# One fetch of v in place of three in the attention of a 12-chunk recurrent kernel, the other two layouts made by TensorE transposes and ScalarE copies

## The chip, the cores and the metric

The kernel runs on one core of a Trainium2 chip. The metric is the time of one execution in microseconds (us); the profile's span leaves out a little at both ends. Engines are named as in the profile: PE (TensorE products; PEld is its weight load), DVE (VectorE), ACT (ScalarE), POOL (GpSimd), SP (SyncE, which here only issues DMAs). Each works through its own list of instructions in a fixed order.

## What is computed

An attention with a recurrent state, over 4 x 8 = 32 heads, 768 time steps and head width 40, and behind it two dense blocks on the 4 x 768 x 320 result:

```python
for t in range(S):                                   # attention; S = 768, state is 40 x 40 per head
    y[:, :, t] = einsum('bhd,bhde->bhe', r_t, state)
    Sa = einsum('bhde,bhe->bhd', state, a_t)
    state = state*w_t - outer(Sa, b_t) + outer(v_t, k_t)
...
mixed = real(fft(fft(x, axis=1), axis=2)); u = x + mixed           # block 1
un = normalise(u); x = u + relu(un @ w_ch1) @ w_ch2                # 320 -> 1280 -> 320
...
u = x + (relu(x^T @ w_tok1) @ w_tok2)^T                            # block 2, over the 768 tokens
out = u + relu(u @ w_ch1) @ w_ch2                                  # 320 -> 1536 -> 320
```

## The kernel before

Attention is cut in 12 chunks (`NSC`) of 64 time steps. The 32 heads and one empty one stand in 11 groups (`NG`) of three, 3 x 40 = 120 partitions. Within a chunk the recurrence becomes products between matrices of 64 steps, and only the 40 x 40 state goes from chunk to chunk. The stages of a chunk, in the order in which `plan` lists them:

- `load`, `decay`, `kg`, `loada`, and `inv` for two chunks at a time: inputs, running products of w (DVE), the products of `am` (a under a head mask) with `bt`, and a triangular inverse of 47 DVE instructions. These run several chunks ahead. The inverse leaves through DRAM (`Ad`, `Md`) and comes back as `AT` and `Mst`.
- `merge`, `kbts`, `pts`: products and transposes that finish the inverse (tiles `mg`, `mc`) and lay out `kbt` and `PT`.
- `load2` (L336): fetches v with time on the partitions, into `LT[64:128]` and once more into `VZt[64:128]`. `load3` (L378): fetches r and v with the head's width on the partitions, into `VZd[:,:,1]`, and makes `rm`, r under three head masks (3 ACT instructions).
- `chain` (L342): the path from chunk to chunk. PE product x (from `RT` and `LT`) to `bdX`, product z, its copies by ACT into `VZt[0:64]`, product s (from `kbt` and `VZt`), and from it the state rows `LT[0:40]` of the next chunk.
- `outp` (L386): transposes st of the state, transposes zt of `VZt[0:64]` into `VZd[:,:,0]`, six products sc of `VZd` with `rm`, their masking, six products y with `kbt`, and `ys`.

`LT`, `r` and `kbt` have two buffers, `VZt`, `VZd` and `rm` one. PSUM has eight banks: 3 for chain and merge ('c'), 2 for kg and sc ('m'), 2 for transposes ('t'), 1 for y.

Among these run jobs for later blocks: the float64 weights are read as integers and turned into pairs of floats (`wdec`, `dec2`; tiles `da`, `mda`, `mdraw`, `mdt`), and behind the attention `fft`, `fft2` (tiles `Xh`, `Xl`, `psA`), the two MLP products (L1050, L1040), the token mixing and the last MLP (L1076).

What sets the order is a written list: `Plan.op` records every operation with an engine, what it reads and what it writes, and `Plan.emit` issues them in the sequence of `ORDER`, a string of base-36 numbers of operations. a suffix `:j` picks a PSUM bank, and an item `+m,bank,j` puts m fill-ins there: products of the identity with itself, whose result nothing reads (`warm`, L52). Every engine keeps to that order, so an instruction that waits holds up all that stands behind it on its engine. The semaphore waits themselves are put in by the framework from the tiles read and written.

Of the kernel before, what the change touches and what calls it, by code (L numbers as in the profile page):

```python
# [29 lines left out]
def layouts(r,k,v,w,a,b):  # L30
    def heads(x,fill=0.0):
        o=np.full((NH,768,D),fill,x.dtype); o[:32]=x.reshape(32,768,D); return o
    def rows(x,fill=0.0):
        h=heads(x,fill).reshape(NG,3,NSC,L,D)
        return np.ascontiguousarray(h.transpose(2,1,4,0,3)).reshape(NSC,120,NG,L)
    out={'rR':rows(r),'vR':rows(v)}
# [10 lines left out]
ATTN=['rR','vR','wR','aR','vT','bkR','hm']  # L47
# [49 lines left out]
class Attn:  # L97
# [232 lines left out]
    def load2(s,i):  # L330
        A=s.A
        s.dma(s.LT[i%2][64:128],A['vT'][i],[],[('LTv',i%2)],1.46,cost=.56,nd=4,bulk=1)
        if i+1<NSC: s.dma(s.VZt[64:128],A['vT'][i],[],['VZv'],1.46,cost=.56,nd=4,bulk=1)

    def chain(s,i):
# [25 lines left out]
        if i+1<NSC:  # L361
            nLT=s.LT[(i+1)%2]; PL=s.RT[(i+1)%NRT]
            for w in range(2):
# [5 lines left out]
                P.op('PE',.638,f,[('kbt',i%2),('VZ',2*w),('VZ',2*w+1),'VZv'],[kp,('LT',(i+1)%2,2*w),('LT',(i+1)%2,2*w+1)],alloc=h[0],cols=1651,cls=1)  # L369
# [8 lines left out]
    def load3(s,i):  # L378
# [3 lines left out]
        s.dma(s.VZd[:,:,1],A['vR'][i],[],['VZdv'],1.92,cost=.95,nd=88,bulk=1)  # L382
        for h in range(3): s.act(.77,s.rm[:,h],r,[('r',i%2),'hm'],[('rm',h)],scale=s.hm[:,h:h+1])

    def outp(s,i):
# [17 lines left out]
        for k in range(6):  # L403
# [4 lines left out]
            P.op('PE',.05+.305*m,f,[('VZd',x) for x in range(2)]+['VZdv']+[('rm',x) for x in range(3)],[ks,('sc',j,0),('sc',j,1)],alloc=hs[0],cols=720*m)  # L408
# [95 lines left out]
    def plan(s):  # L504
# [13 lines left out]
        for w in range(NSC):  # L518
            go(w,'merge','kbts','load2','load3','pts','chain','outp')
# [21 lines left out]
34 85:1 32 35 36 86 37 83 88:1 38 3a 8b:0 89 8y 8e:1 8c 39 3b 8f 3c 94 8k 3d 8l 93 3e 3g 92 3f 8m +7,y,0 95:0 3h 9h:1 96 3i 3j 9e:0 9i 8o 3m 9b:1 3n
9f 8q 3k 98:0 9c 3q 8p ce:1 e6 99 e4 8n 9k:1 3l 8j cg kt 87 cf 84 c1 8a 3o 9l 9p 9o 3p 3s c0 8d e0 dx c2 e1 9n 3t 8g e2 mv 97 3r 9g 3u 3x e5 hr 3v hx
3w 9t e3 hs 9q hw e7 ba ht e8 f3 e9 f2 hy hu b9 +12,y,0 ea:0 my bb 9r eb 9u bd 9v 9w +2,y,0 ej:1 9x ez 9y 9z 9s a0 a1 a2 bc a3 +2,y,0 ed:0 a4 fo a5
be:2 qp ee a6 bf a7 bg 48 ek bh aa bi a8 +2,y,0 ep:0 em:1 a9 eq bj ab ca +3,y,0 bk:0 ae hp ac +1,y,0 bl bm af eg:0 ad bn eh ag f4:1 f5 ah en f6 aj bo
# [763 lines left out]
```

## Time and profile before

| | |
|---|---|
| runs | 968.05, 970.48, 971.21 us; median 970.48 |
| the profiled execution | 967.6 us, its span 965.9 us |
| busy: PE, PEld, DVE, ACT, POOL | 910.0, 842.3, 712.1, 492.1, 374.8 us |
| instructions | 24197, of them 9641 PE products |
| moved by DMA | 146.15 MB, mean 151 GB/s |

The span falls into a start-up (0 to 90 us), the attention (90 to about 380 us), a passage through the FFTs (to 417 us) and the dense blocks (to the end). A busy share over the whole span mixes these; the rows further down are by stretch.

### The profile page before, as it was taken

How to read it: one execution, taken by the hardware profiler on the slowest of the kernel's cores; microseconds unless marked ns; L12 is line 12 of the kernel's file. 1: busy time of each engine (PE TensorE's matmuls, PEld its weight loads, DVE VectorE, ACT ScalarE, POOL GpSimd, SP SyncE). 2: the span in 40 equal slices, each digit the busy share in tenths (PEclk: the TensorE clock that was granted, in tenths of full speed). 3: DMA queues.
4: the chain of work that ended last, by engine and by line, in shares of the span. 5: the costliest groups of instructions: out<-in, count | busy, mean ns of one | idle time of the engine just before them, and what ended most of it. 6: DMA issues, size and time to landing. Idle time of an engine off the chain costs nothing. (4 is left out here: it accounts for less than half of the span.)

```text
span 965.9 us, 24197 instructions
## 1 busy us (share of the span) xinstructions
PE 910.0 (94%) x9641; PEld 842.3 (87%) x9641; DVE 712.1 (74%) x1543; ACT 492.1 (51%) x1068; POOL 374.8 (39%) x504
## 2 busy tenths in 40 slices
PE   7577899999999998799999999999999999999998
PEld 5467788888888887789898988999999999999998
DVE  7699679897968757998979656643786876766554
ACT  5265878888887765443434543323234343433422
POOL 6111614536354445444456553363233313132110
PEclk9688999999999999999999999999999999999999
DMA  9877778899867898755344524459452212303000
GB/s 214 168 150 175 173 160 191 195 220 206 190 168 173 203 268 264 269 177 173 119 163 127 171 75 127 130 154 390 137 182 74 79 52 75 101 1 99 1 29 29
DMA packets 153840, 146.15 MB, mean 151 GB/s; under 512 B 101695, under 2 KB 127359, under 8 KB 152959
## 3 DMA queue, kind: packets, MB, share of 16 engines
q1 hardware_dynamic: 143743, 117.64, 47.1%
q0 software_dynamic: 9984, 26.96, 9.1%
q8 instruction: 76, 1.25, 0.6%
q14 instruction: 37, 0.30, 0.1%
HBM read 96.22 MB, written 43.58 MB: 145 GB/s over the span
## 5 line engine op out<-in xcount | busy, mean ns | idle before, releaser
L1050 PE MATMUL hps<-cc,W1t 128*128 128x512 f32 x480 | 121.0, 396 | 0.9 <-DVE cc L1053 0.8
L1040 PE MATMUL acc<-W,cc 128*128 128x320 f32 x720 | 116.0, 310 | 0.0
L1040 PEld LDWEIGHTS acc<-W,cc 128*128 128x128 f32 x720 | 109.2, 188 | 4.7 <-ACT mdh L839 0.3
L1050 PEld LDWEIGHTS hps<-cc,W1t 128*128 128x128 f32 x480 | 87.8, 188 | 17.8 <-DVE cc L1053 1.1
L1100 POOL TENSOR_TENSOR C<-C,C 128x256 f32<-128x256 f32 x36 | 27.4, 760 | 173.2 <-DVE W1t L1093 115.5
L1052 ACT ACTIVATE cc<-hps 128x512 fp32r<-128x512 f32 x60 | 35.8, 596 | 106.5 <-PE hps L1050 106.5
L1053 DVE SCALAR_TENSOR_TENSOR cc<-hps,cc 128x512 fp32r<-128x512 f32 x60 | 41.3, 689 | 56.3 <-ACT cc L1052 56.1
L54 PE MATMUL warm<-ident 128*128 128x128 f32 x470 | 75.1, 298 | 4.1 <-ACT Xh L886 2.1
L226 POOL TENSOR_SCALAR_AFFINE_SELECT RT<-RT 64x384 f32<-64x384 f32 (+1 forms) x72 | 45.5, 651 | 78.1 <-ACT RT L136 73.6
L216 PE MATMUL kg<-am,bt 120*128 120x192 f32 x242 | 55.2, 363 | 19.3 <-ACT am L136 14.7
L54 PEld LDWEIGHTS warm<-ident 128*128 128x128 f32 x470 | 65.6, 206 | 6.6 <-ACT Xh L886 2.3
L417 POOL TENSOR_SCALAR_AFFINE_SELECT sc<-sc 64x384 f32<-64x384 f32 (+1 forms) x72 | 42.0, 583 | 73.4 <-ACT sc L136 67.2
L1094 DVE TENSOR_TENSOR C<-sb,C 128x256 f32<-128x256 f32 x108 | 44.2, 420 | 33.4 <-PE sb L1087 27.0
L1076 PE MATMUL acc<-v,W1t 128*128 128x320 f32 x432 | 67.4, 309 | 0.0
L1076 PE MATMUL acc<-vb,W1t 128*128 128x320 f32 x432 | 66.9, 309 | 0.0
L1092 ACT ACTIVATE W1t<-C 128x256 fp32r<-128x256 f32 x108 | 42.0, 413 | 45.5 <-DVE C L1094 36.6
L1076 PEld LDWEIGHTS acc<-v,W1t 128*128 128x128 f32 x432 | 63.7, 188 | 0.3 <-DVE W1t L1093 0.3
L1076 PEld LDWEIGHTS acc<-vb,W1t 128*128 128x128 f32 x432 | 63.7, 188 | 0.0
L216 PEld LDWEIGHTS kg<-am,bt 120*128 120x128 f32 x242 | 42.0, 206 | 24.5 <-ACT am L136 15.6
L1093 DVE SCALAR_TENSOR_TENSOR W1t<-C,W1t 128x256 fp32r<-128x256 f32 x108 | 46.6, 449 | 19.5 <-ACT W1t L1092 19.1
L407 PE MATMUL sc<-rm,VZd 120*128 120x192 f32 x264 | 56.7, 344 | 1.4 <-ACT sc L136 0.7
L860 POOL TENSOR_TENSOR mda<-mda,mdh 128x320 f32<-128x320 f32 (+2 forms) x32 | 31.4, 985 | 62.1 <-ACT mdh L857 47.0
(224 smaller groups left out, 2253.5 us busy)
## 6 DMA issues: line engine op xcount, KB each, us to landing
bt<-in_bkR_dram SPq DMA_DIRECT2D x12, 660.0 KB
mdraw<-in_moe_w_ch_dram SPq DMA_DIRECT2D x22, 320.0 KB
mdraw<-in_moe_w_ch_dram SPq DMA_DIRECT2D x16, 384.0 KB
dr_T<-Y SPq DMA_DIRECT2D x24, 256.0 KB
Z<-dr_T SPq DMA_DIRECT2D x6, 1024.0 KB
wS<-in_wR_dram SPq DMA_DIRECT2D x12, 335.2 KB
a<-in_aR_dram SPq DMA_DIRECT2D x12, 335.2 KB
RT<-a SPq DMA_DIRECT2D x36, 111.7 KB
```

What stands on the lines that cost most here:

```text
L54: for x in range(m): nc.tensor.matmul(t[:,128*(x%4):128*(x%4)+128],lhsT=ident,rhs=ident,start=True,stop=True)
L216: nc.tensor.matmul(ps[:,192*x:192*x+192],lhsT=bt[:,g+x].rearrange("p v t -> p (v t)"),rhs=am[:,:,g+x],start=True,stop=True)
L226: nc.gpsimd.affine_select(out=kv,in_=kv,pattern=[[0,3*m],[1,L]],compare_op=ALU.is_gt,fill=0.0,base=0,channel_multiplier=-1)
L407: for x,g in enumerate(gs): nc.tensor.matmul(ps[:,192*x:192*x+192],lhsT=VZd[:,g].rearrange("p v t -> p (v t)"),rhs=s.rm[:,:,g],start=True, ...
L417: nc.gpsimd.affine_select(out=o,in_=o,pattern=[[0,3*m],[-1 if rv else 1,L]],compare_op=ALU.is_gt,fill=0.0,base=L-1 if rv else 0,channel_mu ...
L1040: nc.tensor.matmul(s.pst(acc[x]),lhsT=a[:,sl],rhs=w2(w,m),start=(m==0 and n==0),stop=(m==MT-1 and n==2))
L1050: for n,(l,r) in enumerate(ops): nc.tensor.matmul(ps,lhsT=l,rhs=r,start=n==0,stop=n==7)
L1053: s.dve(.61,lambda: nc.vector.scalar_tensor_tensor(out=t["hl"][z],in0=s.pst(h),scalar=0.0,in1=t["hh"][z].bitcast(F32),op0=ALU.max,op1=ALU. ...
L1076: nc.tensor.matmul(s.pst(acc[x]),lhsT=a[:,sl],rhs=wv(w),start=(u==0 and y==0 and k==0),stop=(u==5 and y==1 and k==2))
L1092: s.act(256,lambda: nc.scalar.activation(out=Hh(y,c),in_=src(),func=AF.Relu),rd,[('Hh',z,y,c)],free=free)
L1093: s.dve(.33,lambda: V.scalar_tensor_tensor(out=Hl(y,c),in0=src(),scalar=0.0,in1=Hh(y,c).bitcast(F32),op0=ALU.max,op1=ALU.subtract),rd+[('H ...
L1094: def add(n,r,m,free): s.dve(.33,lambda: V.tensor_tensor(out=C(n),in0=R[r](),in1=C(m),op=ALU.add),[K[r],('C',m)],[('C',n)],free=free)
```

## The change

The input `vR` (v with the head's width on partitions) is no longer passed to the core, and `VZd[:,:,1]` is made on chip by a new stage `vts`: eleven TensorE transposes of `LT[64:128]` per chunk into a bank 't' (8 and 3 at a time), and two ACT copies from there. The second fetch of v into `VZt[64:128]` becomes two ACT copies from `LT[64:128]`, for every chunk but the last. `warm` issues up to four fill-ins as one product whose right side is the identity repeated along the columns, in the place of one product each. `ORDER` is another list: 4701 operations in place of 4654, with 213 fill-ins in 78 places in place of 235 in 84.

```diff
 def warm(nc,pool,ident,m):
     t=pool.tile([128,512],F32,tag="ps",name="warm")
-    for x in range(m): nc.tensor.matmul(t[:,128*(x%4):128*(x%4)+128],lhsT=ident,rhs=ident,start=True,stop=True)
+    for x in range(0,m,4):
+        k=min(4,m-x); nc.tensor.matmul(t[:,:128*k],lhsT=ident,rhs=ident.unsqueeze(1).to_broadcast([128,k,128]),start=True,stop=True)
...
     def load2(s,i):
         A=s.A
         s.dma(s.LT[i%2][64:128],A['vT'][i],[],[('LTv',i%2)],1.46,cost=.56,nd=4,bulk=1)
-        if i+1<NSC: s.dma(s.VZt[64:128],A['vT'][i],[],['VZv'],1.46,cost=.56,nd=4,bulk=1)
+        for h in range(2 if i+1<NSC else 0):
+            n=slice(17*h,17*h+17-h); s.act(.75,s.VZt[64:128,n],s.LT[i%2][64:128,n],[('LTv',i%2)],[('VZv',h)])
+
+    def vts(s,i):
+        nc=s.nc; P=s.P; LT=s.LT[i%2]; VZd=s.VZd
+        for g in range(0,NG,8):
+            m=min(8,NG-g); h=s.psum('t',[128,512],"vt"); kp=('ps',h[0])
+            def f(g=g,m=m,h=h):
+                ps=s.pst(h)
+                for x in range(m): nc.tensor.transpose(ps[:120,64*x:64*x+64],LT[64:128,3*(g+x):3*(g+x)+3].rearrange("p n d -> p (n d)"),s.ident[64:128,64:128])
+            P.op('PE',.065*m,f,[('LTv',i%2)],[kp,('VZdv',g//8)],alloc=h[0],cols=60*m,cls=3)
+            s.act(.05+.054*m,VZd[:,g:g+m,1],lambda h=h,m=m: s.pst(h)[:120,:64*m].rearrange("p (g t) -> p g t",t=L),[kp],[('VZdv',g//8)],free=[h[0]])
...
     def load3(s,i):
...
         s.dma(r,A['rR'][i],[],[('r',i%2)],1.3,bulk=1)
-        s.dma(s.VZd[:,:,1],A['vR'][i],[],['VZdv'],1.92,cost=.95,nd=88,bulk=1)
...
-            go(w,'merge','kbts','load2','load3','pts','chain','outp')
+            go(w,'merge','kbts','load2','vts','load3','pts','chain','outp')
...
 ORDER="""
-0 1 5 4 7 8 2 6 9 3 1e 1g a 1i 3y 1h 1f 7q 40 41 44 e 42 3z f g 43 45 b c j h 7o +12,y,0 c3:0 fm i bq:1 c4 bx k c5:0 8t l br m 1j bs:1 o n 46 1k d 47
...
```

Products sc now wait for both halves of `VZdv`, and products s for both of `VZv`.

Where the list moves things is seen in three places. First PE from the last sc product of chunk 3's output to the first s product of chunk 4 (z: chunk 4's; y, sc: chunk 3's output; mc: merge of chunk 5; vt: the new transposes, here of chunk 4). Before:

```order
L302 MATMUL mc<-Mst_143,T_147 32x32 x32
L407 MATMUL sc<-rm_140,VZd_141 128x192
L425 MATMUL y<-Sbd_151,r_139 64x120 x2
L429 MATMUL y<-kbt_149,sc_155 64x40 x6
L54 MATMUL warm<-ident 128x128 x2
L356 MATMUL z<-bdX_142,Mst_143 64x80 x16
L425 MATMUL y<-Sbd_151,r_139 64x120 x2
L429 MATMUL y<-kbt_149,sc_156 64x40 x6
L216 MATMUL kg<-am_117,bt_122 128x192 x2
L368 MATMUL s<-VZt_137,kbt_148 40x40 x16
```

and of the change:

```order
L418 MATMUL sc<-rm_140,VZd_141 128x192 x3
L343 MATMUL vt<-ident,LT_135 120x64 x11
L55 MATMUL warm<-ident 128x128
L368 MATMUL z<-bdX_142,Mst_143 64x80 x8
L436 MATMUL y<-Sbd_151,r_139 64x120 x2
L440 MATMUL y<-kbt_149,sc_155 64x40 x6
L368 MATMUL z<-bdX_142,Mst_143 64x80 x8
L436 MATMUL y<-Sbd_151,r_139 64x120 x2
L440 MATMUL y<-kbt_149,sc_156 64x40 x6
L380 MATMUL s<-VZt_137,kbt_148 40x40 x16
```

The eleven transposes stand where the fill-ins and the end of mc stood, and the output's y products go between the two halves of z.

Second, ACT at the same place (`VZt_137<-z`: the copies between z and s). Before:

```order
L136 ACTIVATE Mst_144<-mc 32x16x32 x2
L136 ACTIVATE MT_120<-Mt_119 128x1024
L136 ACTIVATE R_130<-Q_112 120x11
L136 ACTIVATE VZt_137<-z 64x320 x2
L136 ACTIVATE am_117<-a_116,hm_163 120x704 x3
L136 ACTIVATE sc_154<-sc 128x192
L136 ACTIVATE rm_140<-r_139,hm_163 120x704
L136 ACTIVATE VZt_137<-z 64x320 x2
```

and of the change:

```order
L137 ACTIVATE VZt_137<-LT_136 64x640
L137 ACTIVATE Mst_144<-mc 32x16x32 x2
L137 ACTIVATE bdX_142<-x 64x8x40 x2
L137 ACTIVATE R_130<-Q_112 120x11
L137 ACTIVATE sc_154<-sc 128x192
L137 ACTIVATE MT_120<-Mt_119 128x1024
L137 ACTIVATE am_117<-a_116,hm_163 120x704 x3
L137 ACTIVATE VZt_137<-z 64x320 x2
L137 ACTIVATE VZd_141<-vt 120x3x64
L137 ACTIVATE VZt_137<-z 64x320 x2
L137 ACTIVATE RT_132<-kg,sg_164 128x6x64 x2
L137 ACTIVATE VZd_141<-vt 120x8x64
```

One of the new copies into `VZt` stands ahead of z, and the two into `VZd` stand around the second pair of copies from z.

Third, PE ahead of the first product of merge for chunk 2 (mg; it takes `AT_145`, which a DMA brings). Before:

```order
L407 MATMUL sc<-rm_140,VZd_141 128x192 x3
L400 MATMUL zt<-ident,VZt_137 120x64 x11
L292 MATMUL mg<-AT_145,B_146 32x32 x8
L54 MATMUL warm<-ident 128x128 x2
L292 MATMUL mg<-AT_145,B_146 32x32 x24
L54 MATMUL warm<-ident 128x128 x2
L429 MATMUL y<-kbt_148,sc_153 64x40 x6
```

and of the change:

```order
L418 MATMUL sc<-rm_140,VZd_141 128x192 x3
L411 MATMUL zt<-ident,VZt_137 120x64 x11
L55 MATMUL warm<-ident 128x128
L440 MATMUL y<-kbt_148,sc_153 64x40 x6
L343 MATMUL vt<-ident,LT_136 120x64 x11
L356 MATMUL x<-LT_135,RT_133 64x40 x16
L293 MATMUL mg<-AT_145,B_146 32x32 x16
```

A y product, chunk 1's transposes vt and half of chunk 2's x have come ahead of mg.

## Rows read from the trace of the kernel before

**Rows 1.** The page: busy time by engine, TensorE's clock in 40 slices, DMA packets.
```profile
PE 910.0 (94%) x9641; PEld 842.3 (87%) x9641; DVE 712.1 (74%) x1543; ACT 492.1 (51%) x1068; POOL 374.8 (39%) x504
...
PEclk9688999999999999999999999999999999999999
...
DMA packets 153840, 146.15 MB, mean 151 GB/s; under 512 B 101695, under 2 KB 127359, under 8 KB 152959
```

**Rows 2.** Windows by stage: length, PE, PEld, DVE, ACT, POOL busy; clock; DMA share; GB/s.
```profile
0.00:90.00 90.00, 59.42 (x539) 52.38 (x539) 73.96 (x121) 42.83 (x71) 27.68 (x52) 0.83 0.82 184
90.00:118.00 28.00, 24.72 (x505) 21.51 (x498) 22.21 (x45) 24.52 (x44) 13.91 (x23) 1.00 0.67 147
119.00:125.00 6.00, 6.00 (x39) 5.49 (x39) 2.54 (x11) 2.44 (x6) 3.51 (x6) 0.50 0.82 184
126.00:366.00 240.00, 233.55 (x4543) 208.33 (x4542) 190.56 (x372) 194.02 (x372) 110.55 (x165) 1.00 0.87 198
366.00:417.00 51.00, 42.21 (x386) 38.24 (x386) 46.71 (x108) 23.79 (x60) 21.29 (x30) 1.00 0.76 261
417.00:669.00 252.00, 249.65 (x1438) 224.58 (x1438) 178.37 (x376) 93.97 (x209) 119.40 (x127) 1.00 0.52 157
669.00:966.00 297.00, 292.50 (x2175) 289.88 (x2173) 197.79 (x514) 109.03 (x308) 76.70 (x101) 1.00 0.24 80
```

**Rows 3.** PE's waits, 126 to 366 us: total us, times, longest.
```profile
PE y L429 <- POOL sc L417: 1.1, 2, 0.9
...
PE kg L216 <- ACT am L136: 0.5, 1, 0.5
```

**Rows 4.** PE's timeline at 95 us: start, length, instructions.
```profile
95.70 0.68 PE L400 MATMUL zt<-ident,VZt 64*120 64x64 f32 x8
96.31 0.44 PE L302 MATMUL mc<-Mst,T 32*32 32x32 f32 x16
```

**Rows 5.** PE's timeline at 209 and 382 us; these products leave two records each.
```profile
209.18 0.92 PE L407 MATMUL sc<-rm,VZd 120*128 120x192 f32 x4
209.93 0.61 PE L54 MATMUL warm<-ident 128*128 128x128 f32 x4
210.38 0.82 PE L407 MATMUL sc<-rm,VZd 120*128 120x192 f32 x4
...
382.31 2.41 PE L54 MATMUL warm<-ident 128*128 128x128 f32 x20
384.48 0.43 PE L902 MATMUL psA<-T,Xh 128*128 128x416 f32 x1
```

**Rows 6.** Window of the fill-ins' line alone, 90 to 366 us: PE, PEld busy.
```profile
90.00:366.00 276.00, 30.84 (x175) 24.31 (x176) 0.99 0.85 193
```

**Rows 7.** ACT by line and form, 113 to 366 us: count, busy us, mean ns.
```profile
L136 ACT ACTIVATE rm<-r,hm 120x704 f32<-120x704 f32 x33 | 27.8, 875 | 1.2 <-PE sc L407 0.8 <-issue 0.3
...
L136 ACT ACTIVATE VZt<-z 64x320 f32<-64x320 f32 x39 | 16.4, 430 | 5.3 <-PE z L356 4.7
...
L136 ACT ACTIVATE VZd<-zt 120x512 f32<-120x512 f32 x10 | 6.0, 595 | 2.7 <-PE zt L400 2.6
...
L136 ACT ACTIVATE VZd<-zt 120x192 f32<-120x192 f32 x10 | 3.3, 329 | 2.8 <-PE zt L400 2.6
```

**Rows 8.** SP's issues into VZd and VZt: ns min/median/max, first and last.
```profile
L134 SPq DMA_DIRECT2D VZd<-in_vR_dram x12: 877/924/1252, 46.6 to 357.3; - x12
...
L134 SPq DMA_DIRECT2D VZt<-in_vT_dram x11: 498/584/1681, 9.1 to 322.9; - x11
```

**Rows 9.** PE's waits, 90 to 366 us, the only one for a DMA.
```profile
PE mg L292 <- DMA AT<-Ad: 1.5, 1, 1.5
```

**Rows 10.** PE's timeline, 104 to 117 us; in brackets the idle time before.
```profile
104.07 2.57 PE L216 MATMUL kg<-am,bt 120*128 120x192 f32 x12 [1.38 <-DVE sc L412]
...
116.71 0.44 PE L292 MATMUL mg<-AT,B 32*32 32x32 f32 x16 [1.51 <-DMA AT<-Ad]
```

**Rows 11.** PE's timeline at 386 us.
```profile
385.84 0.36 PE L902 MATMUL psA<-T,Xl 128*128 128x208 f32 x1 [0.93 <-DVE Xl L887]
```

**Rows 12.** DVE's timeline at 40 us, where the first inverse begins.
```profile
39.75 0.17 DVE L252 COPY Mt<-N 128x4 f32<-128x4 f32 x1 [4.75 <-DMA N<-Gd]
```

More of the change, by code (lines that the diff above doesn't have):

```diff
@@ L35, in rows @@
         return np.ascontiguousarray(h.transpose(2,1,4,0,3)).reshape(NSC,120,NG,L)
-    out={'rR':rows(r),'vR':rows(v)}
+    out={'rR':rows(r)}
     for i in RV: out['rR'][i]=out['rR'][i][...,::-1]
@@ L407, in f @@
                 for x,g in enumerate(gs): nc.tensor.matmul(ps[:,192*x:192*x+192],lhsT=VZd[:,g].rearrange("p v t -> p (v t)"),rhs=s.rm[:,:,g],start=True,stop=True)
-            P.op('PE',.05+.305*m,f,[('VZd',x) for x in range(2)]+['VZdv']+[('rm',x) for x in range(3)],[ks,('sc',j,0),('sc',j,1)],alloc=hs[0],cols=720*m)
+            P.op('PE',.05+.305*m,f,[(v,x) for x in range(2) for v in ('VZd','VZdv')]+[('rm',x) for x in range(3)],[ks,('sc',j,0),('sc',j,1)],alloc=hs[0],cols=720*m)
             pv=lambda hs=hs,m=m: s.pst(hs)[:,:192*m].rearrange("p (n t) -> p n t",t=L)
@@ L541 @@
[L541 to L544, printed above, removed]
@@ new lines @@
+k7 wh +1,c,0 u6:1 rz n3 rq kd 4z n4 +1,t,0 rs:0 ka nt rv:1 nw p8:0 nz rt nn kb +2,y,0 ps:1 rw rr kc p9 ru s1 pq pt +1,y,0 pa:0 s2 u7 pv px:0 pu pb n6
+pw q8:1 n5 py q6:0 q9 rl tr q0 pc:1 pz wk tn ut:2 pd q1 q7 pe:1 rx uu qd:0 s4 s0 uv wl xm qi:1 pf qe to u8:0 s3 qa:0 tq qf qj ts:1 wi qg wm qb uc tt
+s7 tu wn tv u9 uw:0 tp tx s8 s9 sa xj tw sb ql:1 sc ub 15p sd ty:2 se xk sf tz ux u0 sg s5 uy u1 sh qc:0 ws si s6 sj qh qm sk qr:0 wr sl sm qu:1 u2
+uf:1 sn ud:0 u3 so uk +1,c,0 uz:1 sq ug qo qs qk ue sp qn v1 v2:2 v0 qp ss wt wq v4 wp v5:0 v3 wo x6:0 qv qq qw qx vj:1 v8 x7 x9:1 v6 v9 vk vl:0 sr
@@ new lines @@
+10w:1 yz 54 16u yc yx 10z:0 56 12u 57 yw 12x 10m 110 15s 5c 10x +1,t,1 10t:0 ya 15q 10q:1 51 10u w3 111 zh:1 10r zf:0 10y zi 112:0 10v 55 zg 58 5a
+115:1 113 12z:2 130 116 59 w6:0 yf 119 wb 118 yg z6:0 wc 13o ye wd z1:1 5d wf 5e 11a we yh:1 5g 13b:0 5b 5h yi zj:0 z7 114 16v 13c z9 yj:1 z8 12w
+13d:0 z4 yk za zm:1 5m z2 13e 15t z5 16w zk yl:1 zn 13f:0 z3 11b ym 131 13g 132 12y 117 zb:1 134 zo 15r zp yn:0 133 12v zu:0 15u zc 11d zr:1 ze zd
+140:0 19l yo 16s 15v zv zl:0 15w 13j zq zs zx 160 103:0 zw 100:1 11f 162 11g zt 11h 11i 5f 11j zy 104 11k 13p 11l 13m:1 11m 13k:0 5i 101 13r 135:1 zz
@@ new lines @@
+136 105 13q 11n 106 137 11o 138 13n 102:0 11p 13l 11q 139 143:2 11r 142 11s 11t 107 144 11v 161 17m +1,t,0 179:1 10s 11u 5k 14m:0 108 17a 15x 141
+17b:1 11x 13i 166:0 15y 14p 1cq 5j 11y 163:1 17c 11w 13a 17d:1 5n 145 19n 15z +1,c,1 16x:0 14n 11z 164 5o 17e 109 5q 10b 120 165 10a +8,c,1 146:2 121
+11c 122 149:1 124 16y 11e 14a 123 16z 5r 5p 147 126 +2,y,0 170 14o 5s 16c:1 148 5t 14b 13s:1 14c:2 172 167 14h:1 14f 13t 171 14d 14q:0 14g 14k 16d
+169:0 14i 14r 14l 13u:1 19m 125 16a 173:2 5w 174 17g 127 175 128 176 13v 16i:1 12a 17h 14s:0 129 14e 16f:0 16j 12b 14t 13w:1 16g 12c 155:1 13x 16l 14j
@@ new lines @@
+1zu 21i 2dp 2dq 2de:0 2ds 2df 1zf 1zg 2fv 2ft 2fu 2fw 2fx:1 2dg 2g2:0 1zh 1zl 1zi 1zj 2g0 2fy 2fz 2g1 2g6:1 1z4 1za 1zb 2g3 2g4 2g5 2ex:0 2g7 2g8
+2f0:1 2du 2dv 2dw 2dt 2ey 2ez 2f3:2130 2f4:0 2gz 1zd 1zm 2f1 2f2 2f7 2gy 1zz 2g9 2ga 2f8:1 1zn 1zo 1zv 2f5 2f6 2fb 2fc:0 1zp 1zw 1zx 20a 2gx 1zc 206
+208 1z8 2gb 2gc 2gd 2ge 2gf 2gg 2h4 2h3 2h1 2f9 2fa 2ff 2fg:1 20e 1zy 207 2h2 200 201 202 203 20y 204 2fd 2fe 2fj 2fk:0 205 20f 2fh 2fi 2fn 2fo:1 2h0
+20g 20q 209 20r 20h 20c 20i 20k 20t 218 2fl 2fm 2fr 2he:0 20b 20m 20n 20d 20p 2fp 2fq 2hh 2hb:1 20o 20j 20u 20l 20w 20v 20x 20z 210 212 213 211 21s
@@ new lines @@
+2j7:0 2ja 23l 22x 22y 22z 234 230 231 232 23q 23j 23o 2j8 2j9 2ix:0 2jb 23m 2iv 2iw 2iy 2iz 2jg:1 2jj:0 2jh 23d 23f 233 23r 2jc 235 2jf 241 2jd 23s
+2je 2ji 2jm:2130 2jn:1 242 244 23u 23v 23e 243 248 246 2jk 2jl 2jq 2jr:0 23n 23p 23t 23y 23w 245 247 249 2jo 2jp 2ju 2jv:1 2js 2jt 2jy 2jz:0 2jw 2jx
+2k2 2k3:1 2k0 23x 23z 2gh 2gr 2gi 2gj 2gn 2gk 2go 2gq 2gw 2gp 2gl 2gv 2gm 2gu 2k1 2k6 2k7:0 2gs 2k4 2k5 2ka 2kb:1 2gt 2k8 2k9 2ke 2kf:0 2ko 2kp 2kc
+2kd 2ki 2kg 2kw 2kx 2kh 2kj 2ku 2kv 2ky 2kz 2la:1 2l6:0 2l0 2l2 2l3 2kq 2kr 2l4 2l5 2km 2l1 2l7 2lb 2le 2lf 2li 2lj 2lg 2lh 2kn 2l8 2l9 2lq:0 2lc 2ld
@@ L666 @@
+3ks 3lk 3le 3lo 3ls 3lx 3ly 3lu 3lc 3ld 3l8 3m7 3li 3lt 3lf 3m5 3m6 3lg 3m8 3m2 3lv 3lw 3lz 3m0 3m1 3m3 3m4 3m9 3md 3me 3mb 3mh 3mi 3mc 3mj 3mk 3ma
+3mf 3mg
 """
```

236 lines of the change are left out of this document (110 added, 126 removed).

## The prediction, made before the change was timed

> **What bounds the kernel now.** I read the page first: PE is busy 94% of the span and every other engine less than 75% [rows 1]. That share is a mean, so next the windows by stage [rows 2]. From 126 us to 366 us PE does 233.55 us of work in 240, and behind 417 us it leaves 6.9 us idle in 549. In these stretches the end comes later by what PE is given to do and earlier by what is taken from it. Two stretches are different: the start-up, where PE is idle 30.6 of 90 us, and the passage from 366 to 417 us, where PE is idle 8.8 us and DVE is busy 46.71 of 51. Then PE's own waits [rows 3]: between 126 and 366 us they add up to 6.45 us (240 less 233.55), the longest for POOL's masking of sc, and ACT is named in waits of 0.5 us and less. ACT is busy 194.02 us of those 240, or 81%: not the limit, but with only 46 us free. The DMA engines are busy 87% of that stretch, which looks like the thing to relieve, yet from 90 to 366 us PE waits for a DMA once, 1.5 us [rows 9]. Taking 23 loads away therefore has little to give on PE's path.
>
> **What is removed.** Twelve loads of v into `VZd`, and eleven into `VZt`, with SP's 0.92 and 0.58 us each to issue [rows 8]. PE waits for none of them between 90 and 366 us, so I price them at 0 there. What hides them is that they are issued far ahead of use; what they may be worth in the start-up is the first rival.
>
> **Transposes, +9.4 us.** Each chunk gets eleven of `LT[64:128]`, in the form of the zt transposes (64 rows in, 120 out). Eight of those took 0.61 us from their start to the next product's (95.70 to 96.31 [rows 4]), so eleven take about 0.85. Chunk 0's fall in the start-up where PE idles. Eleven chunks by 0.85 us is 9.4 us, in a stage where PE has no room. The lower end is 0, if all of it stands where PE waited or where a fill-in was dropped.
>
> **Fill-ins, -0.8 us in the attention.** They do no work, so each costs what PE would have done instead, except where PE would have waited. Ten took 2.17 us from their start to the next product (382.31 to 384.48 [rows 5]), 0.22 us each; in the attention 175 records of them fill 30.84 us [rows 6]. A fill-in leaves two records, so these are 88 of them at 0.35 us as records overlap; I take 0.27, between the two ways to count. By the lists there are 92 from the first z to the end of chunk 11's output before and 89 now: 3 x 0.27 = 0.8. Four in one product still have four times the columns, so I price a wide one as four. Were a wide one to cost as one, the 89 in 51 products would be 38 fewer by 0.22, and 8 us would come back; that is the lower end. I do not take it: two sc products of 192 columns took 0.75 us to the next start, two fill-ins of 128 columns 0.45 [rows 5], so PE is paid nearly by the column.
>
> **Ahead of merge(2), -2.5 us.** PE waited 1.38 us at 104.07 and 1.51 us at 116.71, the latter for `AT` [rows 10]. In the new list a y product, chunk 1's transposes and half an x have come ahead of that mg: about 2.6 us of work that has to be done anyway, now in the gap. Bounds: 0 if `AT` comes as much later, -3.2 if all gaps are filled.
>
> **ACT, +2.5 us.** The two copies into `VZt` (64 rows, 680 and 640 elements) have no equal in the trace. Between the copy of 320 elements at 0.430 us and that of 704 at 0.875 [rows 7] a line gives 0.85 and 0.80. The two into `VZd` have the form of zt's: 0.595 and 0.329 [rows 7]. That is 2.57 us a chunk, about 2.2 by start to start, and 22 us over the ten chunks of the stretch: ACT would be busy some 216 of 246 us, 88%. The new order puts one copy into `VZt` ahead of z's copies, and one into `VZd` between the two pairs of them; behind these waits product s, and behind s, on PE, everything. PE's waits for ACT now are below 2 us. I take 2.5 more, nearer to the low end, because the new list gives the copies places between others' waits; the bounds are 0 and 12 (half of the 22 us on PE's path, as the ACT copies between z and s cannot be overlapped with PE at will).
>
> **Clock, -1.5 us.** [...] Bounds: -3, and +3 for each new fall.
>
> **Passage and end, -2 and -1 us.** Between chunk 11's output and the MLP, DVE sets the pace [rows 2], and PE waited 0.93 us for an `Xl` [rows 11] that stood behind weight decoding. By the lists DVE has 81 operations there where it had 89, three of them decoding ones of about 0.45 to 0.9 us: -2, with bounds -4 and +2. Behind 417 us there are 8 fill-ins in place of 15; seven by about 0.2 us is at most 1.5, and I take 1.
>
> **Sum:** 9.4 - 0.8 - 2.5 + 2.5 - 1.5 - 2 - 1 = +4.1 us. On the profiled execution of 967.6 us that is 971.7. The median of the three runs, 970.5, stands 2.9 above that execution, so for a median I predict 970.5 + 4.1 = 974.6 us.
>
> **The rivals.**
>
> *Faster.* Less DMA ahead of the first inverse. DVE waited 4.75 us at 39.75 for `N` [rows 12], in a stretch where the DMA engines moved 184 GB/s [rows 2]. Two loads fewer in the start-up are 660 KB, 3.6 us at that rate. If both pass through, everything behind comes up to 8.3 us earlier: 974.6 - 8.3 = 966. Against it: in SP's new list r(0) is issued ahead, which takes back about half of the bytes, and `N` waits for `Gd`, which waits for PE. It decides if merge(2)'s first product comes before 110 us in place of 116.71. [...]
>
> *ACT becomes the limit.* If the copies meet z's copies in most chunks, the upper end of 12 holds in place of 2.5: 974.6 + 9.5 = 984. For it speaks 88% busy; against it that ACT is free for 46 us now and that PE's longest ACT wait is 0.5.
>
> *No change.* The transposes stand where fill-ins and waits stood: in chunk 4 they take the place of two fill-ins and of the mc products. If four of the 9.4 us go into the 6.45 us of waits, the sum is about 0: 970.5.
>
> [...]
>
> **How the numbers follow.** About 0.3% (2.9 us) is what a measurement of this kernel can tell from no change, so 967.6 to 973.4 is "same". Chances: the forecast 0.42 (its own range 970 to 979; 0.29 of it above 973.4), faster start 0.20, no change 0.20, ACT 0.13, clock 0.05. So slower 0.29 + 0.13 + 0.05 = 0.47, same 0.20 + 0.13 = 0.33, faster 0.20. The range of 966 to 984 leaves out about half of the faster case and a third of the ACT case.
>
> **What would show each step.** In the trace after: vt rows of 8 near 0.6 us to the next product, and PE busy from 126 to 366 us at 97% or more with some 9 us more between z of chunk 1 and z of chunk 11; ACT near 88% there, with PE's waits for ACT under 5 us; a row of four wide fill-ins near 0.87 us; mg's first product within 2 us of 116.7 with less than 1 us of wait; the clock at 1.00 from 100 us on. I am wrong if z to z takes no longer than before (then fill-ins or waits paid for the transposes), if the first mg comes before 110 us, or if PE's waits for ACT exceed 8 us.

## The result, and the profile of the changed kernel

The changed kernel takes 982.33 us in the median of four runs (978.06 to 985.72), the kernel before 969.56 us on the same chip (968.05 to 971.21): a ratio of 1.0129, with a 95% interval of 1.0085 to 1.0173. On another chip it was timed again beside the kernel before: 980.85 against 973.32 us, 1.0065 (1.0029 to 1.0101). It is slower, by more than the +4.1 us of the sum, inside the range.

The profiled execution took 985.72 us, its span 983.7. On its page, PE's busy share is as before and the clock is not [rows 1]:

```profile
PE 926.4 (94%) x9499; PEld 833.0 (85%) x9499; DVE 712.1 (72%) x1543; ACT 519.8 (53%) x1114; POOL 374.3 (38%) x504
...
PEclk9877999799999988999999999999999999999999
```

Before, no slice of TensorE's clock from the fifth on is below 9; here the eighth, the fifteenth and the sixteenth are. Windows cut at the dips say how long (columns as in [rows 2]: stretch, length, PE, PEld, DVE, ACT, POOL busy, clock, DMA share, GB/s):

```profile
90.00:179.00 89.00, 85.33 (x1588) 74.20 (x1586) 72.04 (x138) 79.55 (x150) 44.96 (x66) 1.00 0.69 156
179.00:194.00 15.00, 14.56 (x215) 13.45 (x215) 9.68 (x19) 7.98 (x15) 1.76 (x4) 0.54 0.76 130
194.00:247.00 53.00, 51.66 (x948) 46.01 (x947) 43.33 (x84) 49.27 (x91) 23.18 (x36) 1.00 0.75 169
247.00:252.00 5.00, 4.44 (x30) 4.03 (x31) 5.00 (x11) 3.43 (x7) 0.94 (x1) 0.66 0.29 81
252.00:363.00 111.00, 104.14 (x2048) 88.61 (x2046) 73.48 (x151) 89.14 (x170) 48.82 (x73) 1.00 0.65 161
363.00:375.00 12.00, 10.05 (x111) 7.95 (x112) 8.18 (x12) 3.65 (x9) 7.17 (x11) 0.57 0.74 239
375.00:415.00 40.00, 34.58 (x397) 26.62 (x394) 35.35 (x72) 21.39 (x49) 21.48 (x32) 1.00 0.73 222
415.00:419.00 4.00, 4.00 (x18) 3.81 (x19) 2.52 (x12) 3.01 (x10) 0.00 (x0) 0.57 1.11 413
```

Four stretches between 179 and 419 us were largely at a clock of 0.50 (it reads 0.50 for 180 to 193, 248 to 251, 365 to 373 and 416 to 418 us). A stretch's length times what the clock lacks to 1.00 is what it lost, as far as PE had work: 15 x 0.46 + 5 x 0.34 + 12 x 0.43 + 4 x 0.43 = 15.5 us. Before, the one fall in the attention cost 3 us [rows 2]. Of the 17.8 us by which this span is longer than that of before, then, some 12 are clock. The DMA engines, on the other hand, are less busy than before (0.65 to 0.76 in the long stretches, where [rows 2] have 0.87), and the span is not shorter for it.

What stands ahead of the falls are waits of PE. Its waits from 90 to 380 us (total us, times, longest):

```profile
PE sc L418 <- ACT sc L137: 3.2, 2, 3.0
PE sc L418 <- DVE sc L423: 1.6, 2, 1.4
PE mc L303 <- DMA Mst<-Md: 1.3, 1, 1.3
PE kg L217 <- DVE bt L194: 1.2, 1, 1.2
PE pt L315 <- ACT PT L137: 1.1, 1, 1.1
PE y L440 <- POOL sc L428: 1.1, 1, 1.1
```

They are other waits than those of [rows 3] and [rows 9], and longer: six of over 1 us, where before the two longest were 1.4 and 1.5 [rows 10]. In PE's timeline at the first fall, the wait for `Mst` and the products behind it:

```profile
177.22 0.92 PE L418 MATMUL sc<-rm,VZd 120*128 120x192 f32 x4
179.44 1.89 PE L303 MATMUL mc<-Mst,T 32*32 32x32 f32 x64 [1.31 <-DMA Mst<-Md]
181.26 0.67 PE L436 MATMUL y<-Sbd,r 120*64 120x120 f32 x4
181.72 0.81 PE L440 MATMUL y<-kbt,sc 128*64 128x40 f32 x12
```

Six y products (twelve records) that take 0.50 us elsewhere take 0.81 here. At the second and the fourth fall PE waited too, for DVE:

```profile
247.56 2.74 PE L217 MATMUL kg<-am,bt 120*128 120x192 f32 x8 [1.21 <-DVE bt L194]
...
414.80 4.14 PE L962 MATMUL mix<-T,A 128*128 128x322 f32 x16 [2.35 <-DVE X L965]
```

But not every wait of over 1 us has a fall behind it: those of 1.07 us (ending at 168.13), 1.06 (279.24) and 1.43 (335.95) have none. The longest wait, 3.03 us at 364.94, has a longer history. All engines at that place:

```profile
361.09 0.33 DVE L867 TENSOR_SCALAR mdt<-mdraw 128x320 int32<-128x320 int32 x1 [13.35 <-DMA mdraw<-in_moe_w_ch_dram]
...
361.45 0.49 DVE L868 SCALAR_TENSOR_TENSOR mda<-mdraw,mdt 128x320 int32<-128x320 int32 x1
361.86 0.98 DVE L384 TENSOR_TENSOR LT<-s,LT 40x320 f32<-40x320 f32 x2
...
363.69 0.83 ACT L869 ACTIVATE mdh<-mda 128x320 fp32r<-128x320 f32 x2 [3.66 <-issue]
...
364.42 0.47 ACT L137 ACTIVATE sc<-sc 128x384 f32<-128x384 f32 x1
...
364.94 1.32 PE L418 MATMUL sc<-rm,VZd 120*128 120x192 f32 x3 [3.03 <-ACT sc L137]
```

DVE stood 13.35 us for a piece of weights that was being loaded, with chunk 10's state update (`LT`) behind it; ACT then stood 3.66 us before `mdh`, which reads DVE's `mda` (the profile names no releaser here; in dec_late below the same instruction waits 3.70 us for `mda`), with the copy of sc behind it; and PE stood for that copy. The new list puts the first decoding operations ahead of the state update, and the load (issued at 350 us) only nine operations ahead of them.

Where a run of a kernel was disturbed (over 1.5% above that kernel's fastest), it is left out of the medians, means and ratios here and below.

### The profile page after: what moved, and what is told of

It reads as the page before. It is cut to its first block, busy times and chain, and to the rows that moved or that the text cites. A ratio compares the mean times of both kernels' runs of the same rounds, so it can differ in the third digit from the quotient of the medians.

```text
span 983.7 us, 23898 instructions
## 1 busy us (share of the span) xinstructions
PE 926.4 (94%) x9499; PEld 833.0 (85%) x9499; DVE 712.1 (72%) x1543; ACT 519.8 (53%) x1114; POOL 374.3 (38%) x504
## 5 line engine op out<-in xcount | busy, mean ns | idle before, releaser
L227 POOL TENSOR_SCALAR_AFFINE_SELECT RT<-RT 64x384 f32<-64x384 f32 (+1 forms) x72 | 48.6, 695 | 75.4 <-ACT RT L137 67.7
L55 PE MATMUL warm<-ident 128*128 128x128 f32 (+3 forms) x196 | 69.3, 454 | 4.1 <-POOL ident masks.py:199 2.3
L428 POOL TENSOR_SCALAR_AFFINE_SELECT sc<-sc 64x384 f32<-64x384 f32 (+1 forms) x72 | 38.6, 536 | 71.1 <-ACT sc L137 68.6
L55 PEld LDWEIGHTS warm<-ident 128*128 128x128 f32 x196 | 35.7, 209 | 18.8 <-issue 13.4
```

Of the source, the lines that this page charges most:

```text
L55: k=min(4,m-x); nc.tensor.matmul(t[:,:128*k],lhsT=ident,rhs=ident.unsqueeze(1).to_broadcast([128,k,128]),start=True,stop=True)
L227: nc.gpsimd.affine_select(out=kv,in_=kv,pattern=[[0,3*m],[1,L]],compare_op=ALU.is_gt,fill=0.0,base=0,channel_multiplier=-1)
```

## The experiments

Since runs of one kernel scatter by about 1%, each comparison below also splits the runs in two: span times mean granted clock, an estimate of the span at full clock, and the rest, span times what the clock lacks. The rest holds 15 us that the kernel before loses in the start-up (90 us at 0.83 [rows 2]); in nine other profiles of these runs the start-up has 0.81 to 0.87, 12 to 17 us. Means over the runs (n of them), in us; the kernel before was timed beside each group, 67 runs in all:

| kernel | n | full clock | rest |
|---|---|---|---|
| before | 67 | 947.4 | 23.8 |
| changed kernel (both chips) | 14 | 952.0 | 27.8 |
| single_fill | 3 | 953.0 | 36.0 |
| no_vts | 4 | 949.2 | 31.4 |
| vt_product | 4 | 956.9 | 40.4 |
| dec_late | 9 | 950.3 | 29.3 |
| gaps_filled | 9 | 953.5 | 21.0 |
| no_vzt | 9 | 951.1 | 28.9 |
| order_only | 4 | 948.2 | 35.2 |
| before_wide | 10 | 947.7 | 21.3 |
| before_nofill | 9 | 941.1 | 36.5 |
| before_vts | 9 | 951.6 | 23.9 |
| before_wide_filled | 9 | 946.3 | 19.5 |

Single runs scatter by some 2.5 us at full clock and 4 to 5 in the rest (the 67 of before: 2.5 and 4.2), so a mean over 9 is good to about 1 us in the one and 1.5 in the other. The rest of order_only (runs of 27.3 to 41.5) is good to 3 only, that of single_fill (27.6, 32.5 and 47.9) to 6.

**again.** The changed kernel once more, with no edit.

> The changed kernel itself, once more, beside the three that follow. Theory A (the clock is the loss, by the waits that the new order has): its profile again has stretches at 0.50 between 120 and 380 us, together worth more than 8 us, and the time is 1.0 to 1.6% above before. Theory B (the falls were of that one execution): clock near 1.00 there and 0.5% above before.

980.85 us (10 runs), ratio 1.0065 (1.0029 to 1.0101). The profile again has the clock at 0.50 behind 178, 273 and 362 us, 8.5 us lost there by the same reckoning. The falls are there as theory A has them, so they were not of one execution; but the time, 0.65% above before, is under A's 1.0 and nearer to B's 0.5.

**single_fill.** Every fill-in a product of its own:

```diff
-    for x in range(0,m,4):
-        k=min(4,m-x); nc.tensor.matmul(t[:,:128*k],lhsT=ident,rhs=ident.unsqueeze(1).to_broadcast([128,k,128]),start=True,stop=True)
+    for x in range(m): nc.tensor.matmul(t[:,128*(x%4):128*(x%4)+128],lhsT=ident,rhs=ident,start=True,stop=True)
```

> The changed kernel, with every fill-in a product of its own again (213 products in place of 98); all else as in the change. Theory A (columns): PE pays for a wide fill-in by its columns, so the time stays within 0.3% of the changed kernel's 982 us. Theory B (the wide form lets the clock fall): the stretches at 0.50 near 180, 250 and 365 us go, about 9 us come back, 973 us. A wide product that costs less than its parts would show the other way: up to 8 us slower than 982.

986.54 us (3 runs), ratio 1.0183 (1.0104 to 1.0261): slower, which neither theory had. The third case, a wide product cheaper than its parts, is not the reason: by the split it is 1.0 us more at full clock, no more than the uncertainty, so PE does pay by the column. The other 8 us are clock, but with runs so far apart that three do not show wide fill-ins to be the better ones for the clock. That the wide form brought the falls (theory B) does not hold: none of the three loses clearly less clock than the changed kernel's 27.8.

**no_vts.** No transposes of v, and none of their copies:

```diff
-            P.op('PE',.065*m,f,[('LTv',i%2)],[kp,('VZdv',g//8)],alloc=h[0],cols=60*m,cls=3)
-            s.act(.05+.054*m,VZd[:,g:g+m,1],lambda h=h,m=m: s.pst(h)[:120,:64*m]...
+            P.op('PE',.065*m,lambda: None,[('LTv',i%2)],[kp,('VZdv',g//8)],alloc=h[0],cols=60*m,cls=3)
+            P.op('ACT',.05+.054*m,lambda: None,[kp],[('VZdv',g//8)],free=[h[0]])
```

> The changed kernel without the eleven transposes and the two ACT copies of each chunk that fill the v half of VZd (it holds zeros, so the products sc miss their part from v). Theory A (the transposes' PE time is the loss): 9 to 10 us less, 973 us, with the clock still at 0.50 near 180 and 365 us. Theory B (transposes let the clock fall): the falls go as well, 9 us more, 964 us. Theory C (waits in the new order let the clock fall): no more than A gives, and where PE now runs into the same waits earlier, less than A, 976 to 980 us.

983.11 us (4 runs), ratio 1.0098 (1.0065 to 1.0131), within the uncertainty of the changed kernel and at none of the three times expected. 2.8 us less at full clock, and 3.6 us more clock lost. The transposes are not what lets the clock fall: without them it falls no less. (PE loses their work as well, so this run alone does not say what transposes do to the clock.)

**vt_product.** The transposes as ordinary products:

```diff
-nc.tensor.transpose(ps[:120,64*x:64*x+64],LT[64:128,...],s.ident[64:128,64:128])
+nc.tensor.matmul(ps[:120,64*x:64*x+64],lhsT=LT[64:128,...],rhs=s.ident[64:128,64:128],start=True,stop=True)
```

> The changed kernel with the eleven new transposes of each chunk done as ordinary products with the identity, of the same operands and shapes. [...] Theory B (waits decide the clock): the same falls at the same places and some 4 us more, 986 us.

997.72 us (4 runs), ratio 1.0275 (1.0217 to 1.0333). 4.9 us more at full clock, where theory B has some 4, and 12.6 us more clock lost, where it has the same falls. That the 4.9 come near its 4 is luck: a group takes 2.4 us in place of 0.8, some 18 us more over the eleven groups of the attention, and much of that went into PE's waits (idle 4.9 of 240 us, where the changed kernel has 15.7 in no_vzt's first fence below). PE's timeline (first fence) and the windows around two such groups, then the whole stretch (second):

```profile
111.83 2.37 PE L343 MATMUL vt<-ident,LT 64*120 64x64 f32 x21
114.13 1.13 PE L356 MATMUL x<-LT,RT 128*64 128x40 f32 x32
```

```profile
108.00:114.00 6.00, 5.59 (x69) 5.01 (x64) 4.12 (x8) 5.68 (x10) 4.65 (x9) 1.00 0.74 137
115.00:123.00 8.00, 8.00 (x77) 7.54 (x73) 3.41 (x12) 4.36 (x9) 2.89 (x4) 0.57 0.56 140
...
185.00:190.00 5.00, 5.00 (x62) 4.58 (x58) 4.85 (x9) 4.42 (x8) 1.53 (x2) 1.00 0.91 140
190.00:194.00 4.00, 4.00 (x72) 3.96 (x73) 2.37 (x4) 2.90 (x7) 0.00 (x0) 0.57 0.35 52
...
126.00:366.00 240.00, 235.06 (x4038) 209.99 (x4038) 176.78 (x344) 193.79 (x362) 101.36 (x149) 0.93 0.66 151
```

Here the clock falls to 0.50 right behind 7 of the 11 groups in the attention, and nowhere else from 100 to 400 us, though PE was busy by its records for all of 185 to 190 us and idle for less time (4.9 of 240 us) than in the kernel before. So the fall at 190 us came without idle PE in the 5 us before it: here a stretch of 2.4 us of these small products goes before a fall. What in them matters was not tried.

**dec_late.** The first dozen decoding operations further back in the order (names in place of the list's numbers):

```diff
 ORDER: (dec2's first 12 operations, the state updates of chunk 10, and sc's masking)
-... dec2.DVE0 dec2.DVE1 ... chain10.DVE0 chain10.DVE1 ... dec2.ACT2 ... chain10.DVE2 chain10.DVE3 dec2.ACT0 ... outp10.DVE1 ...
+... chain10.DVE0 chain10.DVE1 ... chain10.DVE2 chain10.DVE3 ... outp10.DVE1 dec2.DVE0 dec2.DVE1 ... dec2.ACT2 dec2.ACT0 ...
```

> The changed kernel with the first dozen operations of the weight decoding dec2 moved in the order from ahead of chunk 10's LT updates to behind chunk 10's second masked sc on DVE; nothing else moves. In the profile DVE stood 13.35 us for the DMA of mdraw, with LT and through ACT's mdh copy a PE wait of 3.03 us behind it, and the clock at 0.50 from 365 to 374 us. Theory A (this wait costs what follows it): the PE wait of 3 us and the fall behind it go, 7 us less, 975 us. Theory B (it is covered by other work): within 0.3% of 982 us.

980.72 us (9 runs), ratio 1.0096 (1.0058 to 1.0135). 1.7 us less at full clock, hardly more than the uncertainty, and the clock falls at the same place (0.51 from 362 to 369 us). The wait was moved, not taken away. In PE's timeline:

```profile
363.90 1.49 PE L303 MATMUL mc<-Mst,T 32*32 32x32 f32 x48 [3.65 <-ACT T L137]
```

ACT stood 3.7 us for the decoding's `mda` as before, now with merge's copy `T` behind it in place of sc's. The time is theory B's, but since the wait is still there neither theory is settled by it.

**gaps_filled.** 47 more fill-ins, ahead of nine instructions for which PE waited; three of the places:

```diff
-... pt ... +1,y,0 pa:0 ...      ... sd ty:2 ...          ... 1kb 1k5:1 ...
+... pt ... +1,y,0 +5,c,0 pa:0   ... sd +6,y,0 ty:2 ...   ... 1kb +13,y,0 1k5:1 ...
```

> The changed kernel with 47 more fill-ins, put where its profile showed PE waiting 0.5 us or more between 165 and 365 us (9 places; about 10 us of fill-ins in 10.8 us of waits). Theory A (the clock falls behind PE's waits): the falls go, the time comes down by 8 to 12 us against the changed kernel, to 0.0 to 0.5% above before, although 47 products more are done. Theory B (the clock falls for the kinds of products, transposes above all): the falls stay and the time is the same or some us longer.

976.52 us (9 runs), ratio 1.0024 (0.9992 to 1.0057): 4 us less than the changed kernel beside it, with more work. Against the ten runs of that (952.5 and 27.0) it is 1.0 us more at full clock and 6.0 us less clock lost, three times the uncertainty: theory A, with about half of its lower end. PE's timeline at the place of the first fall:

```profile
178.48 0.92 PE L418 MATMUL sc<-rm,VZd 120*128 120x192 f32 x4
179.24 1.46 PE L55 MATMUL warm<-ident 128*128 128x512 f32 x4
180.62 1.20 PE L303 MATMUL mc<-Mst,T 32*32 32x32 f32 x64
```

and windows of the same kernel:

```profile
120.00:350.00 230.00, 224.24 (x4189) 193.14 (x4187) 181.31 (x352) 198.98 (x375) 106.76 (x152) 1.00 0.72 164
350.00:363.00 13.00, 10.78 (x133) 7.96 (x128) 4.37 (x11) 6.17 (x14) 3.88 (x7) 0.74 0.82 239
```

The same mc products (64 records) start 1.2 us later than in the changed kernel's profile and take 1.20 us in place of 1.89. The clock holds for 230 us; the fall that is left begins at a wait of 2.2 us that ends at 354.12, which was not among the nine.

**no_vzt.** No ACT copies into `VZt`:

```diff
-            n=slice(17*h,17*h+17-h); s.act(.75,s.VZt[64:128,n],s.LT[i%2][64:128,n],[('LTv',i%2)],[('VZv',h)])
+            s.P.op('ACT',.75,lambda: None,[('LTv',i%2)],[('VZv',h)])
```

> The changed kernel without the two ACT copies per chunk that fill the v half of VZt (it holds zeros, so the products s miss their part from v). 1.65 us of ACT work less per chunk. Theory A (ACT's load makes PE wait): PE's waits between 126 and 376 us shrink from 14.5 to below 9 us, clock falls get fewer, and the time drops by 6 to 10 us against the changed kernel. Theory B (the waits come from the places in the order, not from the load): 0 to 3 us.

981.03 us (9 runs), ratio 1.0098 (1.0062 to 1.0134). ACT's load from 126 to 366 us, here (second line) against the changed kernel in the same session (first line):

```profile
126.00:366.00 240.00, 224.31 (x4125) 195.35 (x4122) 179.01 (x350) 200.33 (x379) 105.66 (x153) 0.96 0.71 163
```

```profile
126.00:366.00 240.00, 225.68 (x4142) 196.88 (x4138) 179.50 (x351) 188.11 (x363) 107.11 (x154) 0.96 0.72 164
```

12 us of ACT work less, the clock as it was, and PE's idle time 14.3 us in place of 15.7. Theory B: the waits come from where things stand in the order, not from how much ACT has to do.

**order_only.** The edits of no_vts and no_vzt together, so that the new order runs without any added work and without 23 loads.

> The new order without any of the added work: no transposes of v, none of the four ACT copies per chunk, and the 23 loads of v left out too (the v halves of VZt and VZd hold zeros, so sc and s miss their part from v). Theory A (the order itself brings the waits that cost clock): span x clock about 947 us, within 2 us of before, but the rest 27 us or more against 24, and the time not below before. Theory B (the added work is the whole loss): as before or some us faster, rest 24 us.

986.02 us (4 runs), ratio 1.0147 (1.0078 to 1.0215). Theory A, and more strongly than expected: at full clock it is as before (948.2 to 947.4), and 11 us more clock is lost. That is also more than the changed kernel loses (27.8), and why is not shown. The longest of PE's waits from 126 to 390 us, and the window:

```profile
PE sc L419 <- ACT sc L137: 4.9, 2, 4.7
PE y L441 <- issue: 4.3, 2, 2.2
...
PE y L437 <- DVE ys L454: 3.1, 2, 2.7
```

```profile
126.00:366.00 240.00, 223.86 (x3936) 194.31 (x3936) 172.21 (x334) 176.53 (x334) 99.45 (x148) 0.91 0.68 155
```

PE is idle 16 of 240 us, where the kernel before leaves 6.45 [rows 2]; the clock is 0.91 there. The changed kernel's profile in the first fence of no_vzt has nearly the same idle time, 15.7 us, at 0.96; so the sum of the waits alone does not set the clock. The order and the missing loads were not taken apart.

**before_wide.** The kernel before with wide fill-ins, the first diff above the other way round.

> The kernel before with one edit: up to four fill-ins as one wide product. Theory A (PE pays by the column): within 0.3% of before. Theory B (a wide one costs clearly less than its parts): up to 8 us faster. Theory C (wide ones hold the clock worse): falls appear between 126 and 366 us, 3 us or more slower.

970.50 us (10 runs) against 973.32, ratio 0.9974 (0.9940 to 1.0008). Full clock 947.7 against 947.4: theory A. The 2.5 us that it seems to gain are clock, and within the interval of nothing.

**before_nofill.** The kernel before without its fill-ins from chunk 0's z to chunk 11's (47 items of `ORDER`, 82 fill-ins).

> The kernel before without the 82 fill-ins that stand between chunk 0's first z and chunk 11's last. Split each run into span x granted clock (what it would take at full clock: 947.4 us in the runs of before so far) and the rest (24 us). Theory A (the fill-ins hold the clock): span x clock falls by some 12 to 18 us (82 by 0.22, less what turns into waits) and the rest grows by as much or more, so that the time is within 0.5% of before or longer. Theory B (the fill-ins are plain cost here): 12 to 18 us faster, 957 us.

979.07 us (9 runs), ratio 1.0064 (1.0020 to 1.0108). 6.3 us less at full clock, half of the lower end of what was expected, and 12.7 us more clock lost. The window:

```profile
126.00:366.00 240.00, 220.70 (x4122) 192.91 (x4122) 183.68 (x356) 183.83 (x352) 103.42 (x155) 0.91 0.83 190
```

Theory A. The fill-ins of the kernel before, which do no work, hold the clock: 1.00 with them [rows 2], 0.91 without.

**before_vts.** Eleven more transposes per chunk in the kernel before:

```diff
                 for x in range(m): nc.tensor.transpose(ps[:120,64*x:64*x+64],VZ[0:64,3*(g+x):3*(g+x)+3]...,s.ident[:64,:64])
+                for x in range(NG if g else 0): nc.tensor.transpose(ps[:120,64*(3+x%5):64*(3+x%5)+64],VZ[0:64,3*x:3*x+3]...,s.ident[:64,:64])
```

> The kernel before with eleven more transposes per chunk, of the form of the change's (they repeat the zt transposes into unused columns of the second zt bank, behind the three that are there; nothing reads them). Theory A (the price of the forecast): 11 or 12 by 0.85 us, span x clock 9 to 10 us longer, 957 us. Theory B (they fall in PE's waits or replace them): less than 5 us. If transposes cost clock, the rest (24 us) grows by 3 us or more.

976.17 us (9 runs), ratio 1.0057 (1.0026 to 1.0088). 4.2 us more at full clock, which is theory B's "less than 5 us", and no more clock lost (23.9 to 23.8). Two of the groups in PE's timeline:

```profile
175.52 0.81 PE L401 MATMUL zt<-ident,VZt 64*120 64x64 f32 x11
176.17 0.64 PE L400 MATMUL zt<-ident,VZt 64*120 64x64 f32 x8
...
199.64 0.81 PE L401 MATMUL zt<-ident,VZt 64*120 64x64 f32 x11
200.38 1.20 PE L292 MATMUL mg<-AT,B 32*32 32x32 f32 x64
```

0.65 and 0.74 us to the next start, some 8 us over twelve chunks. Half of that reaches the end; where the other half went was not traced.

**before_wide_filled.** before_wide with 27 more fill-ins ahead of eight instructions for which the kernel before has PE wait (`+6,y,0` and `+6,c,1` ahead of those of [rows 10], and six smaller ones).

> The kernel before with wide fill-ins and 27 more of them where its profile showed PE waiting 0.5 us or more between 100 and 372 us (8 places). Theory A (waits let the clock fall, fill-ins in them are nearly free): 2 to 5 us faster than before, 969 us where before has 973, by a smaller rest. Theory B: they only add up to 6 us.

965.97 us (9 runs) against 971.46, ratio 0.9959 (0.9924 to 0.9994): just faster than the kernel before, by 1.1 us at full clock and 4.3 us of clock. From before_wide (947.7 and 21.3) it is told apart in neither column, so what the 27 fill-ins add to the wide form is not shown, only that they cost nothing. It has the three fetches of v, the old order, and 27 more products that do nothing.

## Why the prediction was right in its direction and too small

**What failed is the clock step** (-1.5 us; bounds "-3, and +3 for each new fall"). No run shows the -1.5: [rows 2] have 6 us at 0.50 with PE busy throughout, some 3 us lost, and that half of them would come back was the author's estimate. The clock did not come back; it cost 4.0 us more over all runs (27.8 against 23.8) and some 12 in the first profiled pair, of which some 4 come from the profiled execution of the kernel before: it lost only 19.3 us, where that kernel's runs lose 23.8 in the mean. The fall at 119 us did go, as its waits did, and others came where the new order has PE wait. The forecast has a term for the waits that the change removes (-2.5 ahead of merge(2)), and takes PE's waits elsewhere as they were. A falling clock, with a chance of 0.05, is what was measured, and in these runs it does not follow the transposes. Leaving them out did not make it better (31.4 in no_vts and 35.2 in order_only, in place of 27.8), adding as many to the kernel before changed nothing (23.9 to 23.8), and turning them into ordinary products made it much worse (40.4). What these runs show is an order that leaves PE waiting: filling the waits brought 6.0 us back with the transposes in place (gaps_filled), and the order alone, with nothing added, lost 11 (order_only).

In the windows shown, PE's idle time and its clock go together roughly: 6.45 of 240 us and 1.00 before, 5.8 of 230 and 1.00 in gaps_filled, 14 to 16 of 240 and 0.96 in the changed kernel and no_vzt, 16 and 0.91 in order_only (with a wait of 4.7 us), 19 and 0.91 in before_nofill. vt_product is the exception, with 4.9 and 0.93: there the kind of product was changed, and PE waited less.

**The range held by luck.** The measured time lies near the upper end of the range, which stood for ACT as the limit, and no_vzt shows that ACT was not.

**Without the clock the sum was nearly right, in part by luck.** Its other terms add up to +5.6 us; at full clock the runs have +4.6. Two terms were wrong in opposite directions: the transposes were priced too high, and the end behind the first MLP product got longer and not shorter.

- *Transposes, +9.4*: more than twice too much. Adding them costs 4.2 us (before_vts), taking them out with their copies gives 2.8 (no_vts). The duration was nearly right (0.79 us in the changed kernel, 113.60 to 114.39 below; 0.65 and 0.74 in before_vts, in place of 0.85). What was wrong is that all of it would reach the end, "in a stage where PE has no room": only about half did. PE was busy 94% of 126 to 366 us in the changed kernel, and not the 97% or more of the prediction. The sign it named, chunk 1's first z to chunk 11's, took 279.0 us in place of 256.1 (first two lines before, last two after); some 12 of these 23 remain without the clock. Chunk 1's z itself starts 6.2 us earlier, so part of them may be work that the new order has moved behind it; that was not traced.

```profile
107.94 0.75 PE L356 MATMUL z<-bdX,Mst 128*64 128x80 f32 x16
364.08 1.33 PE L356 MATMUL z<-bdX,Mst 128*64 128x80 f32 x32 [0.24 <-ACT Mst L136]
...
101.74 0.77 PE L368 MATMUL z<-bdX,Mst 128*64 128x80 f32 x16
380.77 0.28 PE L368 MATMUL z<-bdX,Mst 128*64 128x80 f32 x1
```

- *Wide fill-ins paid by the column*: right at full clock (947.7 to 947.4 in the old order, 952.0 to 953.0 in the new). Whether they hold the clock better is not shown: 2.5 us less is lost with them in the old order (before_wide), hardly more than the uncertainty, and single_fill's runs are too far apart.
- *Ahead of merge(2), -2.5*: right. The two waits are gone, and mg starts at 115.46 where it started at 116.71 [rows 10], with some 1.6 us of work (a y product and half an x) ahead of it that came behind it before:

```profile
113.60 0.86 PE L343 MATMUL vt<-ident,LT 64*120 64x64 f32 x11 [0.30 <-ACT VZd L137]
114.39 1.13 PE L356 MATMUL x<-LT,RT 128*64 128x40 f32 x32
115.46 0.69 PE L293 MATMUL mg<-AT,B 32*32 32x32 f32 x32
```

- *ACT, +2.5*: the added work is about as priced (27.7 us more busy on the page, where 2.2 a chunk make 26), and it is not the limit: taking the larger half of it out again gave some 1 us at full clock (no_vzt). PE's longest wait for ACT, 3.0 us, is DVE's wait for weights passed on.
- *Removed loads, 0*: right. The DMA share fell from 0.87 to 0.71 in the attention, and order_only, with 23 loads fewer and no work added, is not below before.
- *Passage, -2, and end, -1*: the first right, the second wrong, by the profiles. From chunk 11's first z to the first MLP product (at 431.54 us, before at 417.12) it took 50.8 us in place of 53.0; the rest of the span is 552.2 us in place of 548.8.

**The rivals.** The faster start did not come: mg is 1.25 us earlier, not 7. ACT as the limit is refuted by no_vzt. That the transposes hide (no change) is half true: about half of them did, and the clock made the kernel slower all the same.

**What stays open.** Whether single fill-ins lose more clock than wide ones; why groups of small products go before a fall, and why one wait of 1.2 to 1.4 us does and another does not; whether fill-ins hold the clock better in waits than elsewhere, since no run put as many of them elsewhere; and why the changed kernel lost more clock in the first four runs than in the ten on another chip (29.7 against 27.0, with before at 24.6 there).

## What to carry to other kernels

A wait of PE cost twice here where the clock fell behind it: once as idle time, and again in the slower products that followed (in the changed kernel 1.3 us of wait at 178 us, then 6.9 us of clock, 15 us at 0.54). So price an order by the waits it leaves on that engine, before the work it adds; and compare kernels by span times granted clock and by the rest, for the two move apart. Fill-ins can pay although they do no work: 82 of them were worth 6.4 us net here, and in waits they are nearly free (47 more cost 1.0 us at full clock, 27 more nothing that can be told).

## What was not expected of the hardware

- Eleven 64-column transposes took 0.65 to 0.8 us (before_vts, the changed kernel), the same as ordinary float32 products 2.4 us (vt_product); behind 7 of 11 groups of the latter the granted clock fell to 0.50, without idle time of PE in the 5 us before one of them (windows 185 to 190 and 190 to 194 us of vt_product).
- One product of 512 columns in place of four of 128 changed the time at full clock by 1.0 us or less, in the old order (947.7 to 947.4) and in the new (952.0 to 953.0).
- Executions of one kernel on one chip differ by up to 1.3%: the 29 runs of before beside again have spans of 966.3 to 978.7 us, with mean granted clocks of 0.982 to 0.968.
